# A hand-ordered prologue of attention and weight splitting: fp32 dummy products in front, second pair's scores by unit, and steps moved ahead of the first relu

## The chip, the core and the metric

One core of one Trainium2 chip runs the whole program. The metric is the device time of one execution in microseconds. It was 961.65 us as the median of 3 runs (960.78 to 962.25).

## What is computed

Three layers follow each other: attention in chunks of 32 queries over a short context with memory keys, a two-matrix layer with a squared relu, and a layer of 8 experts of which each token takes one. Only the first two meet the change:

```python
def _attn_ref(q, k, v, mem_k, mem_v):          # 4 x 8 heads x 768 x 64
    ...
        scores = scale * np.matmul(q_c, k_full.transpose(0, 1, 3, 2))
        scores = scores - np.max(scores, axis=-1, keepdims=True)
        a = np.exp(scores)
        a = a / (np.sum(a, axis=-1, keepdims=True) + 1e-09)
        out[:, :, c_start:c_end] = np.matmul(a, v_full)

def _moe_ref(x, w_in, w_out):                  # x: 3072 x 512, d_ff 2048
    h = x @ w_in
    r = np.maximum(h, 0.0)
    g = r * r
    return (g @ w_out).astype(np.float32)
```

## The kernel before

Tokens go in units of 128 and blocks of 256. A `Duo` (line 105) is the attention of a block's two units. Its steps for one unit or both: `scores_mm` (L184, TensorE; records at L161), `scores_max` and `scores_sub` (L188, L192, VectorE; the first unit also needs a small memset, L205), `scores_exp` (L209, ScalarE), `norm` (L213, VectorE: sum, add, reciprocal), `transpose_a_mm` and `transpose_a_copy` (L236, L239; TensorE at L234, ScalarE at L244), `av_mm` (L267, TensorE, again at L161), `av_scale` (L271, VectorE at L274), `transpose_x_mm` (L285), and `transpose_x_hi` and `transpose_x_lo` (L297, L301; ScalarE at L299, VectorE at L303), which leave the attention output as a high and a low part. The pool `ps_a` has one buffer and `ps_y` two, so a pair by unit uses both.

A weight tile of `w_in` (`i0` to `i7`) or `w_out` (`o0` to `o7`) holds two values of f, the index over 16 slices of d_ff. It is loaded by `load_w` (L308) and turned into a high and a low part: `split_w_exp` (L322, ScalarE), `split_w_shift` (L329), `split_w_or` in two steps (L334; records at L339 and L343), all VectorE, `split_w_hi` (L347, ScalarE, a cast) and `split_w_lo` (L354, VectorE, L357). `i0` is done in halves `a` and `b`, and half `a` is all that f = 0 needs. The raw tiles have three buffers, so the load of a tile waits until the `or` of the tile three before it is done. The converted tiles have two.

A `Block` (L369) multiplies: `mm1_products` (L404, records at L410) makes `ph` for one f, `relu` (L415) makes `r`, its square `g` and the parts `gh` and `gl` (ScalarE at L421, L429, L433; VectorE at L435), and `mm2` (L438, records at L446 to L448) adds six products to `y`; the third and the sixth read `gl`. `ph` comes from `ps_h`, which has two buffers; `spin`, into which all dummies are written, holds one of them as long as dummies follow.

From L995 on the order is written out by hand, and each engine runs its own part of it strictly in that order. `keep_busy` (L1016) issues dummy products on TensorE. `hold` (L1002) is a copy of one element on GpSimd into a raw tile, which keeps the load that follows on SyncE's queue from being issued until the named value exists. The prologue treats the first pair `d0` by unit and the second pair `d1` as a whole, splits `i0`, `o0`, `i1` and `o1`, and runs f = 0 and 1 of blocks 0 and 1. Then a loop (L1124) over a planned sequence takes both blocks together for each f from 2 on (`mm1_both`, records at L389), with the weight steps placed at planned numbers in `todo`. `prepare` (L981), planned at number 23, has casts and memsets on GpSimd that need the second part of the constants.

```python
    keep_busy(12)
    d0.scores_mm(u0)
    keep_busy(4)
    d0.scores_max(u0)
    i0t = load_w(*i0, issue=False)
    hold(i0t[:, 1024:].bitcast(F32), d0.mx[u0][0:1, 0, 0:1])
    load_w(*i0, halves=b)
    d1.load_first_qk(0)
    d1.load_first_qk(1)
    load_w(*o0)
    d1.load_first_v()
```

Of the kernel before, what the change touches and what calls it, by code (L numbers as in the profile page):

```python
# [8 lines left out]
F32 = mybir.dt.float32  # L9
# [8 lines left out]
P = 128  # L18
NT = 3072
D = 512  # L20
# [36 lines left out]
def chunk_attention_relu2_moe_top1_kernel(ctx: ExitStack, tc, qk, vv, qt, kv, w_in, w_out, wg, wexp, consts, out):  # L57
    nc = tc.nc
# [8 lines left out]
    tp = ctx.enter_context(tc.tile_pool(name="tp", bufs=4))  # L67
# [11 lines left out]
    ones = cpool.tile([P, P], BF16, name="ones")  # L79
# [226 lines left out]
    raw, converted = {}, {}  # L306

    def load_w(kind, g, halves=None, issue=True):  # L308
        if (kind, g) not in raw:
            raw[kind, g] = kvp.tile([P, 1024, 2], I32, tag="kv", name=f"raw_{kind}{g}")  # L310
        t = raw[kind, g].rearrange("p n two -> p (n two)")
        if not issue:
            return t
        src = (w_in if kind == "i" else w_out)[g].bitcast(I32)
        if halves is None:
            nc.sync.dma_start(t, src)
            return
        for c in halves:
            nc.sync.dma_start(t[:, 1024 * c : 1024 * c + 1024], src[:, 1024 * c : 1024 * c + 1024])


    def split_w_exp(kind, g, halves=None):  # L322
        t = raw[kind, g]
        if (kind, g) not in converted:
            converted[kind, g] = tp.tile([P, 1024], F32, tag="ws", name=f"ws_{kind}{g}", bufs=2)
        for s in slices(halves):
            nc.scalar.activation(converted[kind, g][:, s], t[:, s, 1].bitcast(F32), ACTF.Abs, scale=2.0 ** -111)

    def split_w_shift(kind, g, halves=None):  # L329
        for s in slices(halves):  # L330
            li = converted[kind, g][:, s].bitcast(I32)
            nc.vector.tensor_scalar(li, li, 3, None, op0=ALU.logical_shift_left)

    def split_w_or(kind, g, halves=None, steps=(0, 1)):  # L334
        t = raw[kind, g]
        for s in slices(halves):
            li = converted[kind, g][:, s].bitcast(I32)
            if 0 in steps:
                nc.vector.scalar_tensor_tensor(  # L339
                    li, t[:, s, 0], 29, li, op0=ALU.logical_shift_right, op1=ALU.bitwise_or  # L340
                )
            if 1 in steps:
                nc.vector.scalar_tensor_tensor(  # L343
                    li, t[:, s, 1], -0x80000000, li, op0=ALU.bitwise_and, op1=ALU.bitwise_or
                )

    def split_w_hi(kind, g, halves=None):  # L347
        if (kind, g) not in wh:
            w = wpool.tile([P, 2, 1024], F32R, tag=f"{kind}{g}", name=f"w{kind}{g}")
            wh[kind, g], wl[kind, g] = w[:, 0], w[:, 1]  # L350
        for s in slices(halves):
            nc.scalar.copy(wh[kind, g][:, s], converted[kind, g][:, s])

    def split_w_lo(kind, g, halves=None):  # L354
        for s in slices(halves):
            h, lf = wh[kind, g][:, s], converted[kind, g][:, s]
            nc.vector.tensor_tensor(wl[kind, g][:, s], lf, h.bitcast(F32), op=ALU.subtract)  # L357

    def slices(halves):
        return [slice(0, 1024)] if halves is None else [slice(512 * c, 512 * c + 512) for c in halves]  # L360
# [549 lines left out]
    n = at[2, 0]  # L910
# [8 lines left out]
    for g in range(2, GROUPED - 1):  # L919
        n = at[2 * g, 0]  # L920
# [4 lines left out]
    n = at[NB - 2, 0]  # L925
    plan_gate(NB - 4, n + 3, n + 4, n + 6, n + 9)
    plan_gate(NB - 3, n + 6, n + 8, n + 10, n + 12)
    n = at[NB, 0]
# [21 lines left out]
    for p in range(NP):  # L950
        n = at[NB + p, 0]
# [24 lines left out]
    n = at[NB, 0]  # L976
# [16 lines left out]
        nc.sync.dma_start(ydram[NT : NT + 1, :], zero)  # L993

    with tc.manual_schedule():  # L995
        nc.gpsimd.memset(ones, 1.0)
        d0, d1 = duos[0], duos[1]
        i0, o0, i1, o1, i2, o2 = tiles[:6]
        b0, b1 = blocks[0], blocks[1]
        a, b = (0,), (1,)  # L1000

        def hold(tile_, until):  # L1002
            nc.gpsimd.tensor_copy(tile_[0:1, 0:1], until)
# [9 lines left out]

        spin = ps_h.tile([P, 4, P], F32, tag="h", name="spin")

        def keep_busy(n):  # L1016
            for _ in range(n):
                nc.tensor.matmul(spin, lhsT=ones, rhs=ones.unsqueeze(1).to_broadcast([P, 4, P]), start=True, stop=True)

        u0, u1, other = (0,), (1,), (ps_y, "y")  # L1020
        keep_busy(12)
        d0.scores_mm(u0)
        keep_busy(4)
        d0.scores_max(u0)
        i0t = load_w(*i0, issue=False)
        hold(i0t[:, 1024:].bitcast(F32), d0.mx[u0][0:1, 0, 0:1])
        load_w(*i0, halves=b)
        d1.load_first_qk(0)
        d1.load_first_qk(1)
        load_w(*o0)  # L1030
        d1.load_first_v()
        d0.scores_sub(u0)
        d0.scores_mm(u1, *other)
        d0.scores_exp(u0)
        d0.transpose_a_mm(u0)
        d0.transpose_a_copy(u0)
        keep_busy(3)
        d0.scores_max(u1)
        d0.scores_sub(u1)
        d0.scores_exp(u1)  # L1040
        split_w_exp(*i0, a)
        d0.norm(u0)
        d0.av_mm(u0)
        d0.av_scale(u0)
        split_w_shift(*i0, a)
        split_w_or(*i0, a, steps=(0,))
        d0.transpose_a_mm(u1, *other)
        d0.transpose_a_copy(u1)
        d0.transpose_x_mm(u0)
        d0.transpose_x_hi(u0)  # L1050
        split_w_exp(*i0, b)
        keep_busy(2)
        d0.av_mm(u1, *other)
        d0.transpose_x_lo(u0)
        d0.norm(u1)
        i1t = load_w(*i1, issue=False)
        hold(i1t.bitcast(F32), d0.r[u1][0:1, 0, 0:1])
        load_w(*i1)
        nc.sync.dma_start(cst[:, P:], consts[:, P:])
        d0.av_scale(u1)  # L1060
        keep_busy(5)
        split_w_or(*i0, a, steps=(1,))
        d0.transpose_x_mm(u1, *other)
        split_w_shift(*i0, b)
        split_w_hi(*i0, a)
# [1 line left out]
        split_w_or(*i0, b, steps=(0,))  # L1067
        split_w_lo(*i0, a)
        d0.transpose_x_lo(u1)
        split_w_or(*i0, b, steps=(1,))  # L1070
        d1.scores_mm()
        keep_busy(2)
        b0.mm1_products(0)
        split_w_hi(*i0, b)
        load_w(*o1)
        d1.scores_max()
        split_w_lo(*i0, b)
        split_w_exp(*o0)
        keep_busy(3)
        d1.scores_sub()  # L1080
        b0.relu(0)
        b0.mm1_products(1)
        d1.scores_exp()
        split_w_shift(*o0)
        split_w_or(*o0, steps=(0,))
        keep_busy(3)
        d1.transpose_a_mm()
        d1.norm()
# [11 lines left out]
        d1.transpose_x_mm()  # L1100
        split_w_shift(*i1)
        d1.transpose_x_hi()
        b0.mm2(0)
        d1.transpose_x_lo()
        split_w_exp(*o1)
        b0.mm2(1)
        split_w_or(*i1)
        load_w(*o2)
        b1.mm1_products(0)
        split_w_shift(*o1)  # L1110
        b1.relu(0)
        split_w_hi(*i1)
        b1.mm1_products(1)
        split_w_lo(*i1)
        b1.mm2(0)
        split_w_or(*o1)
        b1.relu(1)
        split_w_exp(*i2)
        split_w_hi(*o1)
# [168 lines left out]
```

## Time and profile before

| what | value |
|---|---|
| median of 3 runs | 961.65 us |
| the profiled execution, its own time | 960.4 us |
| its span, first to last instruction | 958.5 us |
| TensorE busy | 944.5 us (99%) |
| weight loads of TensorE, beside its products | 791.9 us (83%) |
| VectorE busy | 600.7 us (63%) |
| ScalarE busy | 452.2 us (47%) |
| GpSimd busy | 96.2 us (10%) |

The engines are named PE (TensorE; PEld are its weight loads), DVE (VectorE), ACT (ScalarE), POOL (GpSimd) and SP (SyncE, which issues most DMAs). Busy time is that of the recorded instructions; dummies count as busy. An instruction's record runs to its modelled end, so the next one on the same engine can start before it. In a timeline row the square brackets tell how long the engine stood idle before the instruction, and what released it.

### The profile page before, as it was taken

Reading aid. Unit: us, or ns where it says so; the run is one execution under the profiler, and the core shown is the slowest. Engines: PE = TensorE matmul, PEld = TensorE weight load, DVE = VectorE, ACT = ScalarE, POOL = GpSimd, SP = SyncE. Lnnn points to the kernel's source line nnn. Section 1 sums busy time; section 2 is a strip of 40 time slices with the busy share of each in tenths; the row PEclk is TensorE's granted clock in tenths of the full one; section 3 lists DMA queues with packets and bytes.
Section 4 is the critical chain, followed back from the end, with each engine's and each line's share of the span. In section 5 each row is a group of like instructions: output and inputs, shape, how many; then the busy total and the mean of one; then the engine's idle time right before and its main releaser. Section 6 shows DMA issues by size and latency. Waiting matters only on the chain. (4 is left out here: it accounts for less than half of the span.)

```text
span 958.5 us, 19441 instructions
## 1 busy us (share of the span) xinstructions
PE 944.5 (99%) x7862; PEld 791.9 (83%) x7862; DVE 600.7 (63%) x1125; ACT 452.2 (47%) x816; POOL 96.2 (10%) x93
## 2 busy tenths in 40 slices
PE   8999999999999999999999999999999999999997
PEld 5787898888888888888888888888899999888885
DVE  6999653554535444534553464669776666799995
ACT  4686633333233233322332333545444455688885
POOL 0000000000000000000000011012232212112221
PEclk9999999999999999999999999999999999999999
DMA  9466513224020212021100106360886656453631
GB/s 354 174 224 235 170 68 99 77 24 120 23 77 24 97 47 77 24 76 57 50 1 1 45 1 249 133 238 19 335 312 241 231 208 240 186 184 132 220 125 42
DMA packets 30991, 125.51 MB, mean 131 GB/s; under 512 B 8559, under 2 KB 9071, under 8 KB 21554
## 3 DMA queue, kind: packets, MB, share of 16 engines
q1 hardware_dynamic: 25650, 110.30, 32.0%
q0 software_dynamic: 5248, 13.92, 4.0%
q8 instruction: 64, 1.05, 0.5%
q14 instruction: 29, 0.24, 0.1%
HBM read 138.65 MB, written 13.61 MB: 159 GB/s over the span
## 5 line engine op out<-in xcount | busy, mean ns | idle before, releaser
L389 PE MATMUL ph<-xhi,wi 128*128 128x512 f32 x688 | 212.8, 390 | 0.3 <-DVE wi L357 0.3
L421 ACT ACTIVATE r<-ph 128x256 f32<-128x256 f32 x192 | 72.2, 376 | 235.7 <-PE ph L389 201.6
L431 DVE TENSOR_TENSOR g<-r 128x256 f32<-128x256 f32 x160 | 67.8, 423 | 183.5 <-ACT r L421 183.4
L446 PE MATMUL py<-wo,gh 128*128 128x512 f32 x384 | 156.2, 407 | 0.3 <-ACT gh L433 0.3
L389 PEld LDWEIGHTS ph<-xhi,wi 128*128 128x128 f32 x688 | 129.3, 188 | 28.4 <-DVE wi L357 1.2
L448 PE MATMUL py<-wo,gl 128*128 128x512 f32 x384 | 150.4, 392 | 1.1 <-DVE gl L435 1.1
L447 PE MATMUL py<-wo,gh 128*128 128x512 f32 x384 | 150.4, 392 | 0.0
L389 PE MATMUL ph<-xlo,wi 128*128 128x512 f32 x344 | 134.1, 390 | 0.0
L686 DVE TENSOR_TENSOR x<-raw,x 128x1024 fp32r<-128x1024 f32 x88 | 103.2, 1222 | 6.9 <-ACT x L685 5.2
L435 DVE TENSOR_TENSOR gl<-g,gh 128x256 fp32r<-128x256 f32 x192 | 81.5, 425 | 29.9 <-ACT gh L433 8.2
L686 DVE TENSOR_TENSOR p<-raw,p 128x1024 fp32r<-128x1024 f32 x64 | 78.2, 1222 | 22.5 <-ACT p L685 22.4
L685 ACT CAST x<-raw 128x1024 fp32r<-128x1024 f32 x88 | 87.2, 1056 | 0.0
L448 PEld LDWEIGHTS py<-wo,gl 128*128 128x128 f32 x384 | 72.2, 188 | 17.6 <-DVE gl L435 2.3
L446 PEld LDWEIGHTS py<-wo,gh 128*128 128x128 f32 x384 | 72.2, 188 | 16.3 <-issue 2.0
L433 ACT ACTIVATE gh<-r 128x256 fp32r<-128x256 f32 x192 | 79.9, 416 | 10.6 <-PE py L447 2.3
L447 PEld LDWEIGHTS py<-wo,gh 128*128 128x128 f32 x384 | 72.4, 188 | 12.7
L543 POOL DMA_INDIRECT listd<-ent,idx x24 | 24.1, 1004 | 550.3 <-DVE idx L541 339.3
L389 PEld LDWEIGHTS ph<-xlo,wi 128*128 128x128 f32 x344 | 64.6, 188 | 13.4
L685 ACT CAST p<-raw 128x1024 fp32r<-128x1024 f32 x64 | 66.7, 1042 | 1.0 <-DMA raw<-in_wexp 1.0
L835 PE MATMUL po<-x,ht 128*128 128x512 f32 x264 | 65.4, 398 | 0.6 <-DVE ht L825 0.6
L705 POOL DMA_INDIRECT out<-o,slots x27 | 36.3, 1343 | 209.5 <-ACT o L701 91.4
L835 PEld LDWEIGHTS po<-x,ht 128*128 128x128 f32 x264 | 48.1, 188 | 10.1 <-DVE ht L825 1.0
(229 smaller groups left out, 1455.1 us busy)
## 6 DMA issues: line engine op xcount, KB each, us to landing
raw<-in_wexp SPq DMA_DIRECT2D x82, 1024.0 KB
kv<-in_kv SPq DMA_DIRECT2D x19, 880.0 KB
raw_o<-in_w_out SPq DMA_DIRECT2D x8, 1024.0 KB
raw_i<-in_w_in SPq DMA_DIRECT2D x7, 1024.0 KB
ydram<-y SPq DMA_DIRECT2D x24, 256.0 KB
q<-in_qt SPq DMA_DIRECT2D x20, 256.0 KB
qk<-in_qk SPq DMA_DIRECT2D x4, 624.0 KB
v<-in_vv SPq DMA_DIRECT2D x2, 1024.0 KB
```

Source lines behind the costliest of these rows:

```text
L389: nc.tensor.matmul(ph.rearrange("p (s c) -> p s c", s=2), lhsT=w_in_part(w, f, k), rhs=x[:, s, k, :], start=(n == 0), stop=(n == 11),)
L421: nc.scalar.activation(self.r, self.ph, ACTF.Relu, scale=WSCALE)
L431: nc.vector.tensor_tensor(g, r, r, op=ALU.mult)
L433: nc.scalar.activation(gh, r, ACTF.Square)
L435: nc.vector.tensor_tensor(gl, g, gh.bitcast(F32), op=ALU.subtract)
L446: nc.tensor.matmul(self.y[t], lhsT=gh[:, s], rhs=w_out_part(wh, f), start=(f == 0), stop=False)
L447: nc.tensor.matmul(self.y[t], lhsT=gh[:, s], rhs=w_out_part(wl, f), start=False, stop=False)
L448: nc.tensor.matmul(self.y[t], lhsT=gl[:, s], rhs=w_out_part(wh, f), start=False, stop=(f == NF - 1))
L685: nc.scalar.copy(w[:, 0], t)
L686: nc.vector.tensor_tensor(w[:, 1], t, w[:, 0].bitcast(F32), op=ALU.subtract)
L705: nc.gpsimd.indirect_dma_start(out=out, out_offset=bass.IndirectOffsetOnAxis(ap=slots[:, c, 0:1].bitcast(U32), axis=0), in_=self.y[t], in_ ...
L835: nc.tensor.matmul(self.po, lhsT=self.ht[:, part, f, :], rhs=w[:, wp, j * D : j * D + D], start=(f == 0 and part == 0 and wp == 0), stop=( ...
```

## The change

`long`, a tile of 128 x 128 ones in fp32, is set on GpSimd ahead of the bf16 `ones`. `keep_busy` can now use it. In front stand two products of `long` in place of twelve of `ones`; later dummies are fewer too, with one more of `long`. In the first pair, the subtract of unit 0 and the scores of unit 1 come earlier, and the hold of half b of `i0` waits for the maximum of unit 1. `norm` of unit 1 stands ahead of `av_scale` of unit 0, and the exponent step of half a behind both. The hold of `i1` waits for the converted `i0`. The second pair's scores, maximum, subtract and exponential are done by unit. Its second exponential, and the shift and first `or` of `o0`, stand ahead of the first relu. Further on, the `or`s of `i1` and `o1` are taken apart, so that the first `or` of `i1` stands ahead of `transpose_x_lo`, and the first `or` of `o1` and `lo` of `i1` ahead of block 1's first relu.

```diff
+        long = tp.tile([P, D], F32, tag="t2", name="long")[:, :P]
+        nc.gpsimd.memset(long, 1.0)
         nc.gpsimd.memset(ones, 1.0)
...
-        def keep_busy(n):
+        def keep_busy(n, with_=None):
+            x = ones if with_ is None else with_
             for _ in range(n):
-                nc.tensor.matmul(spin, lhsT=ones, rhs=ones.unsqueeze(1).to_broadcast([P, 4, P]), start=True, stop=True)
+                nc.tensor.matmul(spin, lhsT=x, rhs=x.unsqueeze(1).to_broadcast([P, 4, P]), start=True, stop=True)
 
         u0, u1, other = (0,), (1,), (ps_y, "y")
-        keep_busy(12)
+        keep_busy(2, long)
         d0.scores_mm(u0)
-        keep_busy(4)
+        keep_busy(2)
         d0.scores_max(u0)
+        d0.scores_sub(u0)
+        d0.scores_mm(u1, *other)
+        d0.scores_exp(u0)
+        d0.scores_max(u1)
         i0t = load_w(*i0, issue=False)
-        hold(i0t[:, 1024:].bitcast(F32), d0.mx[u0][0:1, 0, 0:1])
+        hold(i0t[:, 1024:].bitcast(F32), d0.mx[u1][0:1, 0, 0:1])
         load_w(*i0, halves=b)
         d1.load_first_qk(0)
         d1.load_first_qk(1)
         load_w(*o0)
         d1.load_first_v()
-        d0.scores_sub(u0)
-        d0.scores_mm(u1, *other)
-        d0.scores_exp(u0)
+        d0.scores_sub(u1)
         d0.transpose_a_mm(u0)
         d0.transpose_a_copy(u0)
-        keep_busy(3)
-        d0.scores_max(u1)
-        d0.scores_sub(u1)
+        keep_busy(2)
         d0.scores_exp(u1)
-        split_w_exp(*i0, a)
         d0.norm(u0)
         d0.av_mm(u0)
+        d0.norm(u1)
+        split_w_exp(*i0, a)
         d0.av_scale(u0)
+        d0.transpose_a_mm(u1, *other)
+        d0.transpose_a_copy(u1)
         split_w_shift(*i0, a)
         split_w_or(*i0, a, steps=(0,))
-        d0.transpose_a_mm(u1, *other)
-        d0.transpose_a_copy(u1)
+        keep_busy(1)
         d0.transpose_x_mm(u0)
         d0.transpose_x_hi(u0)
+        d0.av_mm(u1, *other)
         split_w_exp(*i0, b)
-        keep_busy(2)
-        d0.av_mm(u1, *other)
         d0.transpose_x_lo(u0)
-        d0.norm(u1)
+        d0.av_scale(u1)
+        keep_busy(1, long)
+        split_w_or(*i0, a, steps=(1,))
         i1t = load_w(*i1, issue=False)
-        hold(i1t.bitcast(F32), d0.r[u1][0:1, 0, 0:1])
+        hold(i1t.bitcast(F32), converted[i0][0:1, 0:1])
         load_w(*i1)
         nc.sync.dma_start(cst[:, P:], consts[:, P:])
-        d0.av_scale(u1)
-        keep_busy(5)
-        split_w_or(*i0, a, steps=(1,))
         d0.transpose_x_mm(u1, *other)
...
         d0.transpose_x_lo(u1)
+        d1.scores_mm(u0)
         split_w_or(*i0, b, steps=(1,))
-        d1.scores_mm()
+        split_w_hi(*i0, b)
+        d1.scores_max(u0)
+        d1.scores_sub(u0)
+        d1.scores_mm(u1, *other)
+        d1.scores_exp(u0)
+        split_w_lo(*i0, b)
         keep_busy(2)
         b0.mm1_products(0)
-        split_w_hi(*i0, b)
         load_w(*o1)
-        d1.scores_max()
-        split_w_lo(*i0, b)
+        d1.scores_max(u1)
         split_w_exp(*o0)
         keep_busy(3)
-        d1.scores_sub()
+        d1.scores_sub(u1)
+        d1.scores_exp(u1)
+        split_w_shift(*o0)
+        split_w_or(*o0, steps=(0,))
         b0.relu(0)
         b0.mm1_products(1)
-        d1.scores_exp()
-        split_w_shift(*o0)
-        split_w_or(*o0, steps=(0,))
         keep_busy(3)
         d1.transpose_a_mm()
...
         split_w_shift(*i1)
         d1.transpose_x_hi()
+        split_w_or(*i1, steps=(0,))
         b0.mm2(0)
         d1.transpose_x_lo()
         split_w_exp(*o1)
         b0.mm2(1)
-        split_w_or(*i1)
+        split_w_or(*i1, steps=(1,))
+        split_w_hi(*i1)
         load_w(*o2)
         b1.mm1_products(0)
         split_w_shift(*o1)
+        split_w_or(*o1, steps=(0,))
+        split_w_lo(*i1)
         b1.relu(0)
-        split_w_hi(*i1)
         b1.mm1_products(1)
-        split_w_lo(*i1)
         b1.mm2(0)
-        split_w_or(*o1)
+        split_w_or(*o1, steps=(1,))
         b1.relu(1)
         split_w_exp(*i2)
         split_w_hi(*o1)
```

## Rows read from the trace of the kernel before

**Rows 1.** Windows of the span: length, busy time of each engine (instructions), granted clock, DMA share, GB/s.

```profile
0.00:6.00 6.00, 4.98 (x34) 1.82 (x42) 0.00 (x0) 1.28 (x1) 0.41 (x5) 1.00 0.71 257
6.00:40.00 34.00, 29.86 (x649) 22.09 (x635) 30.61 (x44) 19.32 (x31) 1.82 (x8) 1.00 0.75 287
40.00:70.00 30.00, 30.00 (x133) 24.50 (x132) 28.60 (x37) 24.88 (x47) 0.00 (x0) 1.00 0.59 209
70.00:100.00 30.00, 28.61 (x244) 22.52 (x243) 27.41 (x33) 21.70 (x42) 0.00 (x0) 1.00 0.62 228
```

**Rows 2.** Waits of PE from 60 to 110: us in total, times, longest.

```profile
PE py L448 <- DVE gl L435: 1.1, 2, 0.9
```

**Rows 3.** Timeline of the front: start, us, engine, line, operation, output and input.

```profile
0.75 0.20 POOL L996 MEMSET ones<- 128x128 bf16 x1 [0.29 <-POOLq L1275]
...
1.02 4.88 PE L1018 MATMUL spin<-ones 128*128 128x512 bf16 x12 [1.02 <-POOL ones L996]
...
5.83 0.86 PE L161 MATMUL pss<-qk 64*32 64x64 f32 x64
...
6.72 0.69 DVE L190 TENSOR_REDUCE mx<-pss 128x8 f32<-128x512 f32 x1 [6.72 <-PE pss L161]
7.45 0.69 DVE L195 TENSOR_TENSOR e<-pss,mx 128x512 f32<-128x512 f32 x1
```

**Rows 4.** DMA view of 0 to 7 us: GB/s in 40 equal stretches.

```profile
GB/s 0 0 0 0 0 0 0 0 0 0 228 228 257 257 342 399 456 399 342 428 371 400 456 428 371 371 371 399 428 344 400 304 228 445 237 568 328 468 328 515
```

**Rows 5.** Timeline: the second pair's transposes of `e`, fp32, eight of 128 columns.

```profile
23.68 1.04 PE L234 MATMUL psa<-cst,e 128*128 128x128 f32 x8
```

**Rows 6.** Timeline of VectorE and ScalarE, from the first pair to `o0`.

```profile
11.33 0.69 DVE L274 TENSOR_TENSOR spare_i<-psx,rs 128x512 f32<-128x512 f32 x1 [0.40 <-PE psx L161]
...
13.25 0.68 ACT L327 ACTIVATE ws_i<-raw_i 128x512 f32<-128x512 f32 x1
...
19.35 1.22 DVE L190 TENSOR_REDUCE mx<-pss 128x16 f32<-128x1024 f32 x1
...
22.56 0.69 DVE L332 TENSOR_SCALAR ws_o<-ws_o 128x1024 int32<-128x1024 int32 x1
```

**Rows 7.** Timeline from the first relu to the second pair's `av_scale`.

```profile
21.07 0.36 ACT L421 ACTIVATE r<-ph 128x256 f32<-128x256 f32 x1
...
21.48 0.30 PEld L410 LDWEIGHTS ph<-xhi,wi 128*128 128x128 f32 x2 [0.30 <-ACT r L421]
...
22.33 1.06 ACT L211 ACTIVATE e<-e 128x1024 f32<-128x1024 f32 x1
...
25.03 0.29 POOL L984 CAST before<-cst 128x128 bf16<-128x128 f32 x1 [9.68 <-DMA cst<-in_consts]
...
25.68 0.85 DVE L218 TENSOR_SCALAR sm<-sm 128x16 f32<-128x16 f32 x1
...
25.82 1.48 PE L161 MATMUL psx<-v,spare_o 64*32 64x64 f32 x128 [0.45 <-ACT spare_o L244]
...
28.14 1.22 DVE L274 TENSOR_TENSOR spare_i<-psx,rs 128x1024 f32<-128x1024 f32 x1
```

**Rows 8.** Timeline from the second pair's `xlo` to the end of the first `mm1_both`.

```profile
31.59 1.23 DVE L303 TENSOR_TENSOR xlo<-pst,xhi 128x1024 fp32r<-128x1024 f32 x1 [0.50 <-ACT xhi L299]
...
35.98 0.43 DVE L435 TENSOR_TENSOR gl<-g,gh 128x256 fp32r<-128x256 f32 x1 [0.17 <-ACT gh L433]
...
36.58 0.40 PE L448 MATMUL py<-wo,gl 128*128 128x512 f32 x1
...
36.92 1.23 DVE L357 TENSOR_TENSOR wi<-ws_i,wi 128x1024 fp32r<-128x1024 f32 x1 [0.52 <-ACT wi L352]
...
38.06 1.22 DVE L339 SCALAR_TENSOR_TENSOR ws_o<-raw_o,ws_o 128x1024 int32<-128x1024 int32 x1
...
40.83 0.39 PE L446 MATMUL py<-wo,gh 128*128 128x512 f32 x1
```

**Rows 9.** Timeline of ScalarE: a relu of the planned loop.

```profile
67.21 0.39 ACT L421 ACTIVATE r<-ph 128x256 f32<-128x256 f32 x1 [0.18 <-PE ph L389]
```

## Prediction

> **What bounds the kernel now.** I read the windows of the whole span first, because the diff touches only the hand-written order of the first 38 us. TensorE is busy 30.00 of 30 us from 40 to 70, and 28.61 of 30 from 70 to 100 [rows 1]; most of what is missing there is one wait of 0.9 us for VectorE's `gl` [rows 2]. So from 40 us on a shift of TensorE's stream is passed on to the end at about its own size. Before 40, TensorE is not the bound, since a good part of its busy time is dummy products; VectorE is, with 30.61 of 34 us [rows 1], starting only at 6.72 [rows 3]. One row links the two engines later: at 67.21 ScalarE's relu waits 0.18 us for TensorE [rows 9]. There the weight steps, which ran ahead, are held by TensorE again, so a lead that VectorE wins at the start is not kept to the stage of the 0.9 us wait. What counts is therefore one number: when TensorE has finished the first 12 products of `mm1_both`, that is when the product behind them starts, at 40.83 [rows 8].
>
> **Part 1, the front.** [...] The scores of a unit are 32 fp32 products in the code and 64 in the row [rows 3]: an fp32 product is two such passes. [...] The memset of `long` stands in front of the one of `ones`, at 0.20 [rows 3]; the second is then hidden beside TensorE, and I take the start as unmoved (bounds 0 and +0.1). The scores need `qk`: by the bytes moved, 624 KB are through by about 3.7 us (40 stretches of 0.175 us, added up) [rows 4], and at 5.83 they did not wait for it. [...]
>
> **Part 2, up to the second pair.** From 6.72 to 19.35 VectorE runs 12.63 us [rows 3, 6]. The change reorders the same instructions: both `norm`s come before the first `av_scale`, so the 0.40 us wait for `psx` [rows 6] is filled. I leave 0.05 of it, and the list ends 5.55 + 12.28 = 17.83, a gain of 1.5. The dummies taken out or put in lie beside this, except that they can hold the next TensorE step by 0.2 to 0.9; each such step here has over 0.3 to spare.
>
> The queues moved past: the hold on GpSimd waits for the second maximum, done at about 7.95, instead of the first, which was done at 7.41 [rows 3]; so the five loads behind it on SyncE's queue (`i0` half b, two `qk`, `o0`, `vv`) are issued 0.5 us later. At worst they all land 0.5 later. The first user is the exponent step of `i0` half b, at 13.25 before [rows 6]; its shift, by the lead of 1.5, stands at about 14.9 in the new order, 0.9 after the end of that step, so nothing is lost at that cover. If the cover were gone, it would cost up to 0.5. The hold of `i1` fires at about 15.0 as before, and nothing waits for it until after 25.
>
> **Part 3, the second pair's scores by unit.** One maximum of 1024 takes 1.22 [rows 6]. Halves take 0.69, and the subtract follows the maximum that it needs after 0.73 [rows 3]; where one doesn't need the other I take half of 1.22, 0.60. Maximum, subtract, `lo` of `i0` half b, maximum, subtract: 0.73 + 0.60 + 0.60 + 0.73 + 0.60 = 3.26 from 17.83, so the shift of `o0` starts at 21.08. Before, it was 22.56, behind the first `gl` [rows 6], which now comes after it at 0.34. VectorE is ahead by 1.14.
>
> **Part 4, what is put ahead of the first relu.** The second exponential is released by the second subtract at 21.2 and keeps ScalarE half of 1.06 [rows 7]; only then comes the relu, at 21.73. Before it was at 21.07, and the second group of `mm1` products waited 0.30 for it and started at 21.48 [rows 7]. Behind that relu on ScalarE stand two squares; behind the products on TensorE three dummies, the transposes of `e`, and then `av`. So here the gain of 1.2 us turns into a loss of 0.66: products at 22.14, `av` at 26.48 instead of 25.82, done after 1.48 at 27.96. The exponential itself gains 1.1 us (22.33 to 21.2) [rows 7], but the transposes are behind the products in TensorE's order and can't use it. VectorE's own list would reach `av_scale` at 27.0 (21.08, the 5.58 from shift to scale before, 0.34 for `gl`). A small sum step of 0.85 at 25.68, beside GpSimd's casts that began at 25.03 [rows 7], falls at 24.5, ahead of them, and I take 0.65 off: 26.35. It then stands idle for 1.65 and starts at 28.00 instead of 28.14 [rows 7].
>
> **Part 5, the steps of `i1` and `o1`.** From `av_scale` to the `gl` of block 1, f = 0, VectorE took 28.14 to 35.98. It now does one `or` of `o1` and `lo` of `i1` before that `gl`: 1.14 each, from 36.92 to 38.06 [rows 8]. The first `or` of `i1` moves into the idle 0.50 before `xlo`, and the idle 0.17 before `gl` goes too. So `gl` starts at 28.00 + 7.84 + 2.28 - 0.67 = 37.45, and ends at 37.87. It is needed by the third product of `mm2`, which ran at 36.58 and now waits to 37.91. Four products at 0.226 (133 in 30.00 [rows 1]) are left, so `mm1_both` starts at 38.82 and finds `lo` of `i1` done; twelve products end at 41.53. Before, 16 products from 36.58 would have ended at 40.20; they ended at 40.83 because `lo` of `i1` was late (36.92 plus 1.23, itself 0.52 late on the cast) [rows 8]. So this point is **0.7 later**. The load of `o2` is issued about as before, behind the second `or` of `i1`.
>
> **The sum.** Gained up to the second pair: 1.17 + 0.35 = 1.52. Lost: 0.38 for the halves and 1.00 by the relu's place, which leaves 0.14 at `av_scale`. Then 2.28 lost for two steps ahead of `gl` and 0.67 of idle time gained: `gl` is 1.47 later. Of that, 0.14 was slack ahead of the product that needs it, and 0.63 is the old wait for `lo`, which goes. Net +0.7 us. The profiled execution took 960.4 us, 1.9 more than its span of 958.5; the median of the runs is 961.65. I add to the median, rounding down: 962.3. A measurement of this kernel tells about 0.2%, 1.9 us, from no change, so this is no change.
>
> **Rivals.** (a) The relu does not hold the products. Then nothing but VectorE's own list (26.35) and ScalarE's two relus and copy ahead of `av` set `av_scale`; I take 26.6, and `gl` 1.4 earlier than in the forecast: 962.3 - 1.4 = 960.9. For it: VectorE's and ScalarE's lead is real. Against: the row in which exactly these products wait for exactly this read [rows 7].
>
> (b) As (a), and VectorE's lead is kept to the end of weight splitting, so that the waits of 70 to 100, 1.39 us [rows 1], vanish as well: 960.9 - 1.4 = 959.5, faster. Against: the wait at 67.21 for TensorE [rows 9].
>
> [...]
>
> **How the numbers follow.** The forecast 0.58, (a) 0.18, (b) 0.12, (c) 0.12. Faster is (b), slower is (c), and the rest is the same: 0.12, 0.76, 0.12. The range takes in (a), and VectorE without any idle time (the 1.65 and two or three small gaps gone, 960.2); at the top the late `qk` (scores at 5.8 cost about 1 us) with the small form of (c), 963.9. (b) and (c) are left out.
>
> **What would show it.** Right: VectorE's first maximum near 5.6, and its last `or` of `i0` 1.5 us early, near 17.2; `r` of block 0 near 21.7 and the `mm1` products behind it; over a microsecond of idle VectorE before `av_scale` at 28; TensorE waiting about 1.3 us for `gl` in the `mm2` near 37; the thirteenth product near 41.5. Wrong: `av_scale` well before 27.5; 0.41 us between dummies after 10 us; no wait for `gl`; or a time outside the range with all of this in place, which would mean that the stage from 40 to 100 does not pass the shift on.

## The result and the profile after

The changed kernel took 967.04 us (median of 20 runs, 961.22 to 970.91), the kernel before in the same session 961.49 (20 runs, 959.94 to 963.28). The ratio, by the means, is 1.0054, with a 95% interval of 1.0042 to 1.0066: 5.2 us **slower** (5.55 between the medians). The forecast was 962.3 within 960.2 to 963.9, no change. The profiled execution of the changed kernel took 969.0 us, its span 966.6, so it is 8.1 us longer than that of before (958.5). The time outside the span also grew: it is 2.2 to 2.6 us in all runs of the changed kernel, against 1.9 before. No view shows where this half microsecond goes.

The first view is again the windows. The columns are those of [rows 1]; the two windows from 200 to 210 are new, and for these the kernel before stands below.

The windows of the changed kernel:

```profile
0.00:6.00 6.00, 4.99 (x70) 2.19 (x70) 0.18 (x1) 1.28 (x1) 0.56 (x6) 1.00 0.70 242
6.00:40.00 34.00, 27.32 (x567) 19.95 (x566) 29.80 (x46) 19.05 (x32) 1.96 (x8) 0.95 0.75 286
40.00:70.00 30.00, 30.00 (x134) 24.82 (x133) 27.02 (x34) 23.21 (x44) 0.00 (x0) 1.00 0.53 185
70.00:100.00 30.00, 28.60 (x124) 22.49 (x122) 27.60 (x34) 21.68 (x39) 0.00 (x0) 1.00 0.65 232
200.00:206.00 6.00, 2.68 (x109) 2.01 (x107) 1.61 (x4) 1.50 (x4) 0.22 (x1) 1.00 0.65 35
206.00:210.00 4.00, 3.07 (x32) 2.54 (x33) 2.30 (x2) 0.00 (x0) 0.00 (x0) 0.59 0.35 83
```

The windows of the kernel before:

```profile
200.00:206.00 6.00, 6.00 (x96) 5.03 (x88) 3.23 (x5) 1.83 (x4) 0.00 (x0) 1.00 0.76 54
206.00:210.00 4.00, 4.00 (x20) 3.27 (x19) 3.63 (x8) 0.72 (x3) 0.00 (x0) 1.00 0.16 58
```

From 40 to 100 TensorE is as busy as it was, and what is missing from 70 to 100 is missing in both. The loss is in two other places. One is the prologue, where TensorE is busy 2.5 us less and the granted clock is 0.95 on the mean. The other lies 160 us behind the last line that the diff touches: between 200 and 206 TensorE, which was never idle there, works 2.68 of 6 us, and then has a granted clock of 0.59.

The waits of TensorE name what it waited for. The columns are those of [rows 2].

The waits of TensorE in the changed kernel:

```profile
PE pss L161 <- issue: 6.2, 2, 4.2
PE py L448 <- DVE gl L435: 1.6, 3, 0.9
```

The waits of TensorE in the kernel before:

```profile
PE pss L161 <- issue: 0.7, 1, 0.7
```

"issue" is idle time in which the engine waited for nothing that the profile shows: no semaphore, no buffer, no transfer. There are 5.5 us more of it, and all of it stands inside groups of scores of attention (`pss`): 1.97 us at 19.43 and 4.25 at 206.93. The timeline of TensorE shows the second of these, and the first comes further down.

TensorE's timeline near 200 us in the changed kernel (columns as in [rows 3]):

```profile
201.39 1.29 PE L161 MATMUL pss<-kv,q 64*32 64x64 f32 x102
...
206.93 0.70 PE L161 MATMUL pss<-kv,q 64*32 64x64 f32 x26 [4.25 <-issue]
207.56 0.79 PE L446 MATMUL py<-wo,gh 128*128 128x512 f32 x1
...
209.01 0.63 PE L446 MATMUL py<-wo,gh 128*128 128x512 f32 x1
209.43 0.63 PE L447 MATMUL py<-wo,gh 128*128 128x512 f32 x1
```

The same group in the timeline of the kernel before:

```profile
199.24 1.62 PE L161 MATMUL pss<-kv,q 64*32 64x64 f32 x128
200.79 0.50 PE L446 MATMUL py<-wo,gh 128*128 128x512 f32 x1
```

The scores begin 2.15 us later than before (201.39 against 199.24): that is the loss of the prologue, 2.54 us where it ends, 2.2 from 49 us on, and passed on from there for 150 us. From their start to the product behind them it is now 6.17 us instead of 1.55, because the run of 128 records stops after 102 and stands still. Then six products, at half the granted clock, start some 0.43 us apart instead of 0.23, which is 1.2 us more. So 2.15 + 4.62 + 1.2 = 8.0 of the 8.1 us. The thirteenth product of the first `mm1_both`, the number on which the forecast stood, started at 43.37 (the 2.54 us); forecast 41.53, before 40.83 [rows 8].

### The profile page after: what moved, and what is told of

The parts are those of the page before. It is cut to its first block, busy times and chain, and to the rows that moved or that the text cites. A ratio compares the mean times of both kernels' runs of the same rounds, so it can differ in the third digit from the quotient of the medians.

```text
span 966.6 us, 19415 instructions
## 1 busy us (share of the span) xinstructions
PE 945.8 (98%) x7847; PEld 793.0 (82%) x7847; DVE 600.1 (62%) x1127; ACT 452.4 (47%) x817; POOL 95.4 (10%) x94
```

## The experiments

**Theory 1** is that TensorE ran out of instructions, because its instruction stream has moved. The profile counts 7847 products of TensorE where it counted 7862, and as many weight loads: the change issues 30 instructions fewer, all of them in the prologue (an fp32 product counts as two: the two long dummies in front are x4 in the timeline of the prologue further down). From there on every instruction of TensorE stands 30 places earlier in the program. The profile lists a DMA queue for instructions, and theory 1 assumes that TensorE gets its instructions in the packets of this queue.

The changed kernel, DMA queues (packets, MB, share of 16 engines' span):

```profile
q8 instruction: 63, 1.03, 0.5%
```

That is 16 KB a packet, and in this trace 1.13 us on the mean. From 40 to 70 us no cost of a packet shows: one moves from 61.70 to 62.60, and TensorE is busy 30.00 of 30 us. Theory 1 says that it is otherwise in one place: the scores of a pair are 128 products in the profile's count with 128 weight loads, 256 instructions in 1.55 us, whereas a big product with its weight load takes 0.226 us [rows 1]. That a packet can come too late for so dense a group is the author's assumption, which the runs are to test. **Theory 2**, the rival, is that the new order itself, with the clock that follows from it, costs the time. In the experiments a tiny product is a bf16 one of 8 columns into a buffer that is overwritten afterwards; 15 of them take 0.5 us (0.53 in e1 and in e5).

**e1 and e2: the number of instructions restored in the prologue.** In the changed kernel, 15 tiny products behind the scores of unit 1 (e1), or between the first relu and the `mm1` products behind it (e2).

```diff
+        def pad(n):
+            for _ in range(n):
+                nc.tensor.matmul(spin[0:32, 0, 0:8], lhsT=ones[:, 0:32], rhs=ones[:, 0:8], start=True, stop=True)
...
         d0.scores_mm(u1, *other)
+        pad(15)
```

> The changed kernel with 15 tiny products (32 x 8) added to TensorE's queue behind the second scores, where TensorE stands idle for 1.2 us. Theory 1, instruction supply: TensorE's instructions come in packets of 16 KB (the instruction queue of the profile); the change took 15 products out of the stream, which moved a packet's border into the dense run of score products at 201 us, and TensorE ran dry there. The padding puts every later instruction back where it was: no idle of 4 us near 203, at most 1 us of waits put down to issue on scores, time 961 to 962.5, and a spread over the runs of about 3 us as before the change. Theory 2, the new order and its fewer dummies cost the time (the clock): it stays at 966 to 968, spread 10 us.

> The changed kernel with the same 15 tiny products, but right ahead of the second group of mm1 products near 22 us, where TensorE waits for the relu anyway. Theory 1: the wait near 203 us goes, the one in the second pair's scores at 17 to 19 stays, since it lies ahead of the padding; 962 to 964. Theory 2: 966 to 968.

964.70 us, ratio 1.0037 (1.0025 to 1.0048), and 964.67, 1.0045 (1.0031 to 1.0059). Near 200 us nothing stands still any more. But a new hole is there in both, in the second pair's transposes of x. The timeline of e1:

```profile
29.83 0.55 PE L234 MATMUL pst<-cst,spare_i 128*128 128x128 f32 x3
33.53 0.77 PE L234 MATMUL pst<-cst,spare_i 128*128 128x128 f32 x5 [3.15 <-issue]
```

Three of eight transposes of one group run, and the other five, which need nothing more, start after 3.15 us of idle time. In e2 it is 2.71 us at the same place, and in both a stretch at half clock follows (34 to 38 in e1: 0.59). So moving the stream back cures the place at 200, as theory 1 says, and the tiny products in the prologue open another hole. Both times lie between the ranges of the two theories; the timeline decides.

The place in the stream alone does not explain the new hole. With the tiny products put in, 602 products stand ahead of these transposes, as many as in the kernel before, where they run through:

```profile
29.41 1.09 PE L234 MATMUL pst<-cst,spare_i 128*128 128x128 f32 x8 [0.93 <-DVE spare_i L274]
```

In the trace of before a 16 KB packet of instructions had ended 1.5 us ahead of this row (27.93); in e1 it moved from 31.29 to 32.24, while TensorE stood still.

**e3: the order of before, with 30 instructions fewer.** The twelve dummies in front become three long ones, which count as six, and nine are saved behind them; not a step is moved.

```diff
-        keep_busy(12)
+        keep_busy(3, long)
...
-        keep_busy(4)
+        keep_busy(1, long)
...
-        keep_busy(5)
+        keep_busy(1, long)
+        keep_busy(1)
```

> The kernel before, its order untouched, with 30 TensorE instructions fewer: the twelve dummies in front become three fp32 ones (5.1 us either way), four and twice four later ones become one fp32 one each, and three dummies go. Theory 1: it gets slower like the changed kernel, 964 to 968, with waits for issue in the scores near 17 or near 200. Theory 2: as before the change, 961 to 962, as the order is untouched and TensorE is kept busy as long.

965.45 us, 1.0051 (1.0037 to 1.0065), 5.2 us above the before of its session (960.28): nearly the whole loss, without any of the new order. The big products run with those of before to 0.15 us until 200 us, and then, in the timeline of e3:

```profile
199.10 1.26 PE L161 MATMUL pss<-kv,q 64*32 64x64 f32 x100
203.43 0.81 PE L161 MATMUL pss<-kv,q 64*32 64x64 f32 x28 [3.06 <-issue]
204.16 0.79 PE L446 MATMUL py<-wo,gh 128*128 128x512 f32 x1
```

The same run of scores stops at nearly the same record (100 here, 102 in the changed kernel). This is the run that decides: theory 2 has nothing to offer for it.

**e4: the front alone.** The kernel before with two long dummies in place of the twelve and 8 tiny products, which keep the number of instructions.

```diff
-        keep_busy(12)
+        keep_busy(2, long)
...
         d0.scores_mm(u1, *other)
         d0.scores_exp(u0)
+        pad(8)
```

> The kernel before with the two fp32 dummies in front in place of twelve, and 8 tiny products behind the second scores so that the stream keeps its length; the order untouched. Theory 1: VectorE starts 0.9 us earlier, its list up to the second pair runs through, 960.4 to 961.3. Theory 2, the shorter front costs the clock: 963 or more.

960.34 us, 1.0000 (0.9991 to 1.0009). VectorE starts at 5.62 instead of 6.72, and in the profile TensorE's later products come 0.8 to 1.1 us earlier (the scores near 200 at 198.28), but the median of the runs shows none of it.

**e5: the number restored where no dense group of small products follows soon.** In the changed kernel, 15 tiny products ahead of the `mm2` of block 1, f = 0, at 36.7 us.

```diff
+            if (b, f) == (1, 0):
+                for _ in range(15):
+                    nc.tensor.matmul(self.y[0][0:32, 0:8], lhsT=ones[:, 0:32], rhs=ones[:, 0:8], start=True, stop=True)
```

> The changed kernel with the 15 tiny products ahead of block 1's first mm2, near 38 us, where TensorE waits for gh and gl. Theory 1 (instruction supply): the stream up to 38 us is as in the changed kernel, so no dry spell in the transposes at 30 us as the earlier paddings had; from 38 us on it is as in the kernel before, so none near 203. What stays is the prologue, some 2 us later than before the change: 962 to 963.5. Theory 2 (order and clock): 966 to 968.

961.06 us, 1.0014 (1.0005 to 1.0023), less than had been expected, and 0.9 us above the 960.19 of before in its session. 30 instructions that do nothing take about 4.7 of the 5.5 us away (967.04 less 961.49, less the 0.9 that is left). Neither the hole near 200 nor that near 30 is there. Of the 0.9 us that are left, 0.4 lie in the span (medians of 958.7 and 958.3) and 0.5 outside it. The prologue now runs by the steps of the forecast, as the next section shows.

**e6, e7, e11: the two costs of the forecast taken back.** On top of e5: the first relu and its products ahead of the second exponential (e6); the `or`s of `i1` and `o1` and `lo` of `i1` in their old places (e7); both (e11).

```diff
+        b0.relu(0)
+        b0.mm1_products(1)
         d1.scores_exp(u1)
         split_w_shift(*o0)
         split_w_or(*o0, steps=(0,))
-        b0.relu(0)
-        b0.mm1_products(1)
```

```diff
-        split_w_or(*i1, steps=(0,))
         b0.mm2(0)
...
-        split_w_or(*i1, steps=(1,))
-        split_w_hi(*i1)
+        split_w_or(*i1)
...
-        split_w_or(*o1, steps=(0,))
-        split_w_lo(*i1)
         b1.relu(0)
+        split_w_hi(*i1)
         b1.mm1_products(1)
+        split_w_lo(*i1)
         b1.mm2(0)
-        split_w_or(*o1, steps=(1,))
+        split_w_or(*o1)
```

> As the kernel padded at 38, with the first relu and the second mm1 products put back ahead of the second exponential and the steps of o0. By the prediction's step that the relu holds these products, they start up to 0.6 us earlier and the time falls by 0.5 to 1 against the kernel padded at 38. Rival: the first mm1 products themselves come so late (TensorE ran dry in the second pair's scores at 17 us) that the relu's place no longer matters: within 0.3 of it.

> As the kernel padded at 38, with the steps of i1 and o1 from the second pair's transpose_x_hi on in the order of before. By the prediction's step that two steps ahead of block 1's gl hold mm2, the wait for gl goes and the time falls by 0.4 to 1 against the kernel padded at 38. Rival: the wait for lo of i1 comes back in its place at equal size: within 0.3.

> The changed kernel with the 15 tiny products in the second mm2, the first relu and its products put back ahead of the second exponential, and the steps of i1 and o1 in the order of before. By the walk of the prediction the two costs of 1.0 and 2.3 us at VectorE go, the gain in front stays: the product behind the first twelve of mm1_both starts 0 to 0.6 us after that of the kernel before, at most where lo of i1 allows, time 959.5 to 960.5. If the remaining loss of some 0.8 us comes from the front (a late half of i0, the second pair by unit), nothing is won over the single undoings: 960.7 to 961.3.

961.31 us, 1.0010 (1.0001 to 1.0019); 960.75, 1.0005 (0.9996 to 1.0014); 960.67, 1.0007 (0.9999 to 1.0016). Taking the tail back gains perhaps 0.3 us, taking the relu back nothing that can be seen, and both together do not go below the kernel before, though the front should have left a gain. None of the three is clear of e5 by the intervals, so the gains that the walk promised (0.5 to 1 us in e6) are not found. The windows of e11 show what stood against them in its profiled execution:

```profile
18.00:20.00 2.00, 1.88 (x67) 1.26 (x65) 1.97 (x4) 0.91 (x2) 0.00 (x0) 0.64 1.03 434
20.00:22.00 2.00, 2.00 (x11) 2.00 (x10) 1.50 (x3) 1.39 (x2) 0.00 (x0) 0.51 0.98 409
```

And the timeline of e11, TensorE and ScalarE:

```profile
16.31 0.85 PE L161 MATMUL pss<-qk 64*32 64x64 f32 x64 [1.35 <-DMA qk<-in_qk]
17.81 1.43 PE L161 MATMUL pss<-qk 64*32 64x64 f32 x64 [0.66 <-DMA qk<-in_qk]
...
20.64 0.63 PE L410 MATMUL ph<-xhi,wi 128*128 128x256 f32 x2
21.07 0.41 PE L410 MATMUL ph<-xlo,wi 128*128 128x256 f32 x1
21.28 0.63 PE L410 MATMUL ph<-xhi,wi 128*128 128x256 f32 x2
...
22.51 0.38 ACT L421 ACTIVATE r<-ph 128x256 f32<-128x256 f32 x1 [1.13 <-PE ph L410]
```

The second pair's scores now wait for `qk`, 2.0 us in all, and then the granted clock falls to half for a stretch around 20 us, in which the `mm1` products start 0.64 us apart instead of 0.36. The relu comes at 22.51, 1.4 us later than before [rows 7], although nothing stands ahead of it on ScalarE. Seven of the ten profiles with the new front and the new treatment of the second pair (the changed kernel, e2, e6 to e8, e11, e12) have this stretch of half clock around 20 us (granted 0.60 from 20 to 23 in the changed kernel, 0.58 from 18 to 22 in e12); e5 does not have it (1.00 from 6 to 40), though up to 36 us it is the changed kernel instruction by instruction, so it comes and goes from one execution to the next. None of the four profiles with the order of before (before, e3, e4, e10) has it.

**e8 and e9: is a transfer beside the scores to blame?** Beside the hole near 200 run the loads of the next pair's q. e8 plans them two numbers later.

```diff
-            plan(s + 1, duos[b + 1].load_q, 0)
-            plan(s + 1, duos[b + 1].load_q, 1)
+            plan(s + 3, duos[b + 1].load_q, 0)
+            plan(s + 3, duos[b + 1].load_q, 1)
```

> The changed kernel, no padding, with the two loads of q of every later pair planned two steps later, so that they no longer fall on the instruction packet of 2.9 us at 203. Theory 1 with contention: the packet takes about 0.9 us there, the idle time near 203 falls from 4.2 to about 2 us, the time to 964 to 965.5. Theory 1 without contention: the idle time stays near 4 us, the time at 966 to 968.

967.58 us, 1.0078 (1.0065 to 1.0092), with a hole of 3.60 us, and a miss: SyncE's queue runs ahead of the plan, and the load was still issued in the middle of the scores, as soon as these freed the buffer of q (200.91, with the scores from 200.02). e9 holds it instead by a copy of one element on GpSimd that needs the pair's maximum.

```diff
             self.q[t] = qp.tile([P, 4, P], F32, tag="q", name=f"q{u}")
+            if u >= EARLY + TPB:
+                nc.gpsimd.tensor_copy(self.q[t][0:1, 0, 0:1], duos[self.b - 1].mx[BOTH][0:1, 0, 0:1])
```

> The changed kernel, with the load of the next pair's q held until the maximum of the present pair exists, so that it no longer moves beside the scores of the present pair. Instruction supply alone: the position in TensorE's stream is as in the changed kernel, the dry spell of some 4 us in the scores near 201 stays, time 966 to 968. Instruction supply slowed by the other transfer: the packet there takes about 0.9 us instead of 2.9, the dry spell shrinks to between 0.5 and 2 us, time 963 to 965. The new order as the only cause: no change, 967.

965.51 us, 1.0060 (1.0046 to 1.0074). Now the load is issued behind the hole, and the hole is smaller, but there. The timeline of e9, and the DMA view of its stretch 200.0 to 204.2:

```profile
199.78 1.15 PE L163 MATMUL pss<-kv,q 64*32 64x64 f32 x95
203.30 0.56 PE L163 MATMUL pss<-kv,q 64*32 64x64 f32 x33 [2.36 <-issue]
...
205.52 0.80 SPq L136 DMA_DIRECT2D q<-in_qt  x2
```

```profile
DMA packets 1, 0.02 MB, mean 4 GB/s; under 512 B 0, under 2 KB 0, under 8 KB 0
...
q8 instruction: 1, 0.02, 3.2%
```

The packet of instructions is the only transfer in these 4.2 us, and its 3.2% of 16 engines are 2.2 us; in the changed kernel it was 2.93, beside the load. So the load is not the cause of the hole. Whether it makes the hole longer is not shown: it is 2.36 us here, and 3.06 (e3), 3.60 (e8) and 4.25 beside the load, in one profile each. The length of the packet, the hole and the time all lie between the two expectations.

A slow packet does not tell the kernels apart either. In all fourteen traces one of 2.2 to 3.1 us moves near these scores, in the kernel before from 200.63 to 203.43, and there nothing stops. Its DMA view from 199 to 205:

```profile
q8 instruction: 1, 0.02, 2.9%
```

In the four kernels that stop, this packet starts 0.35 to 1.0 us after TensorE has stopped, and in e3 and e9 TensorE goes on before the packet has ended (203.43 and 203.75; 203.30 and 204.10).

**e10: the order of before, with 30 instructions more.** 15 tiny products ahead of the twelve dummies.

```diff
+        pad(15)
         keep_busy(12)
```

> The kernel before with 15 tiny dummy products more behind the twelve in front, which moves all later TensorE instructions by 30 places the other way and costs about 0.5 us before VectorE starts. Instruction supply: the places that run dry are other ones; either none is hit (960.3 to 961.3), or a dense run of small products is hit somewhere (2.5 to 4 us of idle TensorE, 963 to 965); a shift of the stream by 2 us or more appears at one place only, as a step. Theory 2, order and clock: nothing but the 0.5 us, 960.3 to 961.

962.35 us, 1.0033 (1.0020 to 1.0046). The front starts 0.7 us later, and one step of 1.6 us is added, at a place that runs through in every other kernel. The timeline of e10:

```profile
116.35 0.39 PE L389 MATMUL ph<-xhi,wi 128*128 128x512 f32 x1
118.16 0.39 PE L389 MATMUL ph<-xhi,wi 128*128 128x512 f32 x1 [1.42 <-issue]
```

So it is not that the changed kernel has a bad number and before a good one of few: each of the shifts tried here has its own places. This hole stands in the big products, some 2.5 us behind a pair's `av`, and not in a dense group, as had been expected; and it is shorter than the 2.5 to 4 us.

No packet of instructions runs in this hole, but one ends 1.53 us before the hole does (116.63). The early holes end alike, by the packets and product counts in the traces. The 17 "issue" holes of over 0.4 us ahead of 120 us, in twelve of the fourteen kernels, all end 1.24 to 1.54 us behind the end of a 16 KB packet. They stand at the same counts, with 222, 349 or 350, 605 or 1241 products ahead of them, whatever work a kernel has there; a kernel does not stop at every one of them.

**e12: half the padding.** As e5, with 8 tiny products.

```diff
-                for _ in range(15):
+                for _ in range(8):
```

> The changed kernel with 8 instead of 15 tiny products in the second mm2, so that TensorE's later instructions stand 14 places ahead of those of the kernel before. Instruction supply: the border of a packet still falls in the scores near 201, later in them by 16 instructions; a dry spell of 1 to 4 us remains there if the border still comes ahead of the run's last products, time 963 to 967; none if the place is already behind them, 961. Theory 2, order and clock: 967 as the changed kernel, since 7 tiny products do no work that matters.

961.67 us, 1.0017 (1.0008 to 1.0026). No hole; the scores near 200 run through in e12:

```profile
199.95 1.51 PE L161 MATMUL pss<-kv,q 64*32 64x64 f32 x128
```

14 places ahead of before are harmless, 30 are not: a jump, which no amount of work saved or added explains. Eight tiny products, which do nothing and take some 0.3 us, decide some 4 us (5.55 above before for the changed kernel, 1.57 here, each in its session).

## Why the prediction was wrong

**The walk through the prologue held in e5.** e5 has every edit of the change, and its stream has the old length where it leaves the prologue. Its steps beside the forecast, in us:

| step | before | forecast | e5 | changed kernel |
|---|---|---|---|---|
| VectorE's first maximum | 6.72 | 5.55 | 5.95 | 5.82 |
| last `or` of `i0` | 18.75 | 17.2 | 17.34 | 17.66 |
| first `r` of block 0 | 21.07 | 21.73 | 21.85 | 23.45 |
| `mm1` products behind it | 21.48 | 22.14 | 22.27 | 23.88 |
| second pair's `av` | 25.82 | 26.48 | 26.60 | 28.21 |
| its `av_scale` | 28.14 | 28.00 | 28.12 | 29.73 |
| `gl` of block 1, f = 0 | 35.98 | 37.45 | 37.53 | 39.12 |
| `mm2` product that needs it | 36.58 | 37.91 | 38.00 | 39.60 |
| thirteenth product of `mm1_both` | 40.83 | 41.53 | 41.76 | 43.37 |

The timeline of e5 shows the two steps on which it turned, the relu that holds the products and the idle VectorE behind it:

```profile
21.85 0.37 ACT L421 ACTIVATE r<-ph 128x256 f32<-128x256 f32 x1
22.27 0.50 PE L410 MATMUL ph<-xhi,wi 128*128 128x256 f32 x2 [0.62 <-ACT r L421]
...
28.12 1.23 DVE L274 TENSOR_TENSOR spare_i<-psx,rs 128x1024 f32<-128x1024 f32 x1 [1.61 <-PE psx L161]
```

0.62 us of wait for the relu, and 1.61 of idle VectorE where the forecast had 1.65. The sum was +0.7; the thirteenth product of e5 came 0.93 later. That the median of e5 is 0.9 above before as well is partly luck: in its profile 0.6 of the 0.93 are left at 49 us and 0.1 at the end of the span, while 0.5 us lie outside the span, where the prediction had no term. Rivals (a) and (b) fall with the second of these rows.

For the rest of this section, the timeline of the changed kernel's prologue (TensorE, VectorE and ScalarE):

```profile
1.01 3.78 PE L1021 MATMUL spin<-long 128*128 128x512 f32 x4 [1.01 <-POOL long L997]
4.72 1.06 PE L161 MATMUL pss<-qk 64*32 64x64 f32 x64
5.82 0.69 DVE L190 TENSOR_REDUCE mx<-pss 128x8 f32<-128x512 f32 x1 [5.82 <-PE pss L161]
...
17.19 0.27 PE L161 MATMUL pss<-qk 64*32 64x64 f32 x2 [0.66 <-DMA qk<-in_qk]
19.43 1.16 PE L161 MATMUL pss<-qk 64*32 64x64 f32 x62 [1.97 <-issue]
...
23.45 0.38 ACT L421 ACTIVATE r<-ph 128x256 f32<-128x256 f32 x1 [0.74 <-PE ph L410]
```

**Part 1, the front.** Two long dummies are the first row, four products in the profile's count: an fp32 product of 512 columns is two passes. The next instruction starts 3.71 us after the first, so a long dummy takes 1.85 us. No run shows the forecast's term for the front, a gain of 1.17 us with VectorE's start at 5.55; it was the author's estimate. With 1.85 us for a long dummy and scores of 0.86 to 1.19 us, VectorE's first maximum came 0.8 to 1.1 us earlier (e5, the changed kernel, e4). The term was right to 0.4 us.

**The step that failed** stands in the first paragraph of the prediction: "from 40 us on a shift of TensorE's stream is passed on to the end at about its own size". In time it nearly is, up to 200 us (2.54 us at 43, 2.15 at 199). But the change also moved the stream by 30 places, and this was costed at nothing: by "The dummies taken out or put in lie beside this" (part 2) they count only as time beside other work, not as instructions. The missing term is 4.62 us of idle TensorE in the scores near 200 and 1.2 at half clock behind it, in the profiled execution; in the medians it is about 4.7 (e5 against the changed kernel), and e3, which moves no step, loses 5.2 to it. The prediction named a time outside the range as a sign, but gave it no chance, and would have put it down to the stage from 40 to 100, which passes the shift on.

**The rest of the prologue's loss**, 2.54 us in the profiled execution where 0.7 was forecast, lies ahead of the relu. The hole of 1.97 us in the second pair's scores was 0.73 before and is 1.26 in e5. From 20 to 23 us the granted clock is 0.60, and now the relu waits for `ph`, not the products for the relu. So the place of the relu, which the forecast priced at 1.0 us, cost nothing in this execution: something later had taken its place. And a cover had been missed. The five loads behind the hold were costed at nothing with `i0` half b as their first user; the first to wait is the second pair's scores, 0.66 us for `qk` in these rows and 1.35 and 0.66 in e11.

**Rival (c)**, with a chance of 0.12, named the right side, slower. TensorE ran at half clock for a stretch of the prologue (granted 0.60 from 20 to 23 us), but this wasn't the cause of the 5 us. Where the half clock comes alone (e6, e7, e11, e12), the time is 960.7 to 961.7, inside the forecast's range. Behind the hole near 200 it adds 1.2 us. The top of the range, 963.9, was put together from a late `qk` at the first scores and a small form of (c), and no run shows either term: the first scores of the changed kernel start at 4.72, 3.71 us behind the start of its long dummies, and the highest median with the half clock alone is 961.7.

**What stays open.** That the number of TensorE's instructions ahead of the scores near 200 decides whether they stop is shown (e3, e5, e12): the four kernels with 30 fewer stop there, the ten others do not. For the early holes and e10's, a packet of instructions that comes late is the likeliest reading, as they all end 1.24 to 1.54 us behind a packet. For the hole near 200 this is only argued, and the packet beside it speaks against it. That hole has 2284 to 2291 products ahead of it in all four, and this count falls inside the same scores in the ten others too, near record 85 in the kernel before and 92 in e12. So, in the terms of theory 1, the border of a packet is not simply moved into the group, and why 14 places are harmless is not settled. Nor is it settled why the granted clock falls near 20 us in some profiles and not in others, or what the half microsecond outside the span is.

## What to carry to other kernels

Where an engine runs a long program without a loop, count the instructions that a change adds or removes, not only their time: here, moved by 30 places, a dense group of small ones stood still for 2.4 to 4.3 us, 160 us behind the edit, and moved the other way, a group of big ones for 1.4 us (e10). Before a reordering is judged by its time, look for "issue" among the waits of the engine that bounds the kernel, and run the change once more with its instruction count restored by a few tiny instructions, at more than one place, since e1 and e2 opened a new hole and e5 did not; only what is left then is the price of the new order. A dummy that keeps an engine busy has a place in the stream too, and taking it out was not free even where its time was hidden: e3, with fewer dummies and no step moved, lost 5.2 us.

## What the runs showed of the hardware that was not expected

- A group of scores, 256 instructions in 1.5 us, stops after 95 to 102 of its 128 records for 2.36 to 4.25 us, without any wait, in four kernels (the changed one, e3, e8, e9), and always the same group; in the ten others it runs through.
- A packet of 16 KB of instructions takes 1.13 us on the mean of the span, but 2.2 us near 200 with no other transfer moving (e9), and beside the load of q 2.93 in the changed kernel and 2.8 in the kernel before, where nothing stops.
- Behind each of these holes, and those in the transposes of e1 and e2, TensorE had half its clock for a stretch: granted 0.59 from 206 to 210 in the changed kernel, 0.57 from 203 to 207 in e3, 0.59 from 34 to 38 in e1, 0.50 from 34 to 40 in e2; in e8 and e9 the big products start 0.43 us apart for a stretch instead of 0.23. In the changed kernel that is 1.2 us on top of 4.25. Behind the 1.42 us of e10 it stayed at 1.00.
- The changed kernel's runs spread over 9.7 us (961.22 to 970.91), those of before over 3.3, of e5 over 1.7. The lowest run of the changed kernel is within 0.2 us of the median of e5, so the holes do not seem to be of one size in every execution; only the profiled one shows them.
- VectorE's small sum step took 0.85 us beside GpSimd's casts [rows 7], and 0.17 in e5, where it ended within 0.1 us of their start, as the forecast had taken it.
